# Loading x as float16 through GpSimd's queue and reordering the first loads of a state-space and feed-forward kernel

## The chip, the core and the metric

The kernel runs on one core of a Trainium2 chip. The metric is the device time of one execution in microseconds (us); lower is better. The time before is a median of 125.82 us over 3 runs (125.32 to 125.95). The profile is of one execution on that core.

The names of the engines in the profile: PE is TensorE's matmul and PEld its weight load, DVE is VectorE, ACT is ScalarE, POOL is GpSimd and SP is SyncE, which does nothing here but issue transfers. A "q" behind the name (SPq, POOLq) is the engine's sequencer, issuing or waiting.

## The reference

Two layers, one behind the other. The first is a chunked state-space scan over 4 batches, 8 heads and 768 tokens, with a head dimension of 32 and a state of 16. The second is a bilinear feed-forward over all 3072 tokens, with a model width of 256 and an inner width of 1536.

```
log_a = log(clip(a, 1e-6, 1))
for each chunk c of the sequence:
    cum   = cumsum(log_a of the chunk)
    L     = exp(cum_i - cum_j), causal
    y     = ((C B^T) * L) x  +  (C state) * exp(cum_i)
    state = exp(sum log_a) * state + sum_j exp(cum_last - cum_j) B_j x_j
X   = y as (batch * token, head * dim)           # 3072 x 256
out = ((X w_a) * (X w_b)) w_out                  # 3072 x 256, float32
```

All inputs and the output are float32 in DRAM. The inputs x, B and C lie as (batch, head, token, element), so one token of one head is a contiguous run of 128 bytes of x and of 64 bytes of B or C.

## The kernel before, in words

**Work items.** The kernel cuts the 768 tokens into 6 blocks of Q = 128 tokens and the 4 batches into 2 pairs of batches. A "pair" p, from 0 to 11, is one block of two batches: block p // 2, batches 2 (p % 2) and the next one. Pairs 0 to 3 (p below P0 = 4) hold two neighbouring tokens of a head on one partition, so their x comes in runs of 256 bytes and each pair is loaded by two transfers of 64 partitions each, one for each batch (`load1`). Pairs from 4 on hold one token on each of 128 partitions, and one transfer loads the whole pair (`load2`).

**A pair's steps.** The decay factors come from scans over a (`scan`, `factors`). `scale_bc` multiplies B and C of a pair by them into float16 tiles bm and cm. For pairs 0 to 3 PE transposes them (`transposes`, evacuated by ACT into bt and by DVE into ct); from pair 4 on they go into a tile "planes", which a transposing DMA on SP turns (`turn`, tile "turned"). `scores` multiplies C and B on PE, `mask` multiplies the scores by the causal mask on DVE (or, with `by_pool`, ACT copies them to tmp and POOL multiplies), and the float16 result t is the moving operand of `pv_u`, whose stationary operand is the pair's x in float16, the tile X16. `ds_mm` multiplies bm and X16 into the state's increment; `state_sums` (DVE) and `state_spread` (POOL: tiles spair or sbd, and gU) carry the state on. Pairs 0 to 3 go through `pv`; from pair 4 on both pairs of a block go through `outputs` in `group(blk)`.

**x.** Before the change x is loaded as float32 (tile xn) and `scale_x` makes X16 from it, multiplying by XS = 1024: on ACT for pairs 0, 1, 2, 5 and 6 and on POOL for pairs 3, 4 and 7 to 11. Evacuations of y multiply by YS / XS, with YS = 16, to undo the factor.

**Feed-forward.** `unit` (pairs 0 to 3, 256 tokens at a time) and `bunit` (a block of 512 tokens) multiply Wa and Wb with y on PE into the PSUM tiles aps and bps; ACT copies aps into asb and DVE multiplies bps and asb into hk or hkb; `out_mm` or `bout` multiplies that with Wo, ACT evacuates into osb and SP stores it. The weights are float32 in DRAM and arrive as float16 by transfers that POOL issues, in two halves each (`load_w`, `load_wo`): half 0 of Wa and Wb in the head of the program, half 1 and Wo later.

**What sets the order.** Nothing is scheduled by a compiler (`tc.manual_schedule()`): each engine runs its instructions in the order in which the program text issues them, and waits on semaphores for what others make. A transfer is an instruction of the engine that issues it: SP, ACT or POOL. So a load in POOL's list is issued only when POOL has done everything that stands ahead of it, and holds up what stands behind it for as long as its issue takes. The built program uses eight semaphores in turn for transfers of SP and ACT together, and eight for those of POOL; a transfer waits for the one that used its semaphore before.

**The head.** SP and ACT issue a and the loads of pair 0, a table ch (head and parity masks) and a table c32; POOL makes sel, ident and causal, then issues three of the four loads of B and C of pair 1, Wa and Wb half 0, and both loads of x of pair 1. PE runs warm-up matmuls on zeros (`warmup`, tile warm) between the steps of pair 0. The feed-forward starts with `unit_mm(0, 0, Wa)`: L600 in the profile, the first instruction to need a weight.

**Later loads.** `loads_bc` issues C and B of a pair on SP. x of pairs 3, 4, 6, 7, 9, 10 and 11 is issued on SP, and of pairs 2, 5 and 8 on POOL. `prep(p)` is `scale_bc` of both on POOL, then `turn`; `prep_x(p)` is `scale_x` on POOL.

Of the kernel before, what the change touches and what calls it, by code (L numbers as in the profile page):

```python
# [10 lines left out]
f32 = mybir.dt.float32  # L11
f16 = mybir.dt.float16
# [16 lines left out]
def kernel(  # L29
# [34 lines left out]
    for b in range(nb):  # L64
        p32[b * H : (b + 1) * H, 128 + b * NG : 128 + (b + 1) * NG] = 1.0
    p32_t = nc.inline_tensor(p32, "p32")
    ph = np.zeros((128, H + 2), np.float32)
    ph[:, 0:H] = (j[:, None] // N) == np.arange(H)[None, :]
    ph[:, H:] = (j[:, None] // N) % 2 == np.arange(2)[None, :]
    ph_t = nc.inline_tensor(ph, "ph")  # L70

    const = ctx.enter_context(tc.tile_pool(name="const", bufs=1))
    c32 = const.tile([BH, p32.shape[1]], f32, name="c32")
    ch = const.tile([128, H + 2], f32, name="ch")
    ident = const.tile([128, 128], f16, name="ident")
    causal = const.tile([128, 2, Q], f16, name="causal")
    sel = const.tile([BH, 2, NBP, H], f32, name="sel")
    indm = c32[:, 0:128]
    selb = c32[:, 128 : 128 + nb * NG]
    headm = ch[:, 0:H]  # L80
    par = ch[:, H:]

    big = ctx.enter_context(tc.tile_pool(name="big", bufs=1))
    a_sb = big.tile([BH, NBLK, Q], f32, name="a_sb")
# [21 lines left out]
    G = big.tile([128, nb, NG], f32, name="G")  # L106

    inp = ctx.enter_context(tc.tile_pool(name="inp", bufs=3))
    mid = ctx.enter_context(tc.tile_pool(name="mid", bufs=4))
    ffh = ctx.enter_context(tc.tile_pool(name="ffh", bufs=4))  # L110
    hkb = ctx.enter_context(tc.tile_pool(name="hkb", bufs=2))
# [9 lines left out]


    pair_in = {}
    banks = iter(BANKS)

    def bank(name):
# [3 lines left out]
    def tiles(p):  # L130
        Bn = inp.tile([128, H, 2, N], f32, name="bn", tag="bn")
        Cn = inp.tile([128, H, 2, N], f32, name="cn", tag="cn")
        Xn = inp.tile([128, H, 2, D], f32, name="xn", tag="xn")
        pair_in[p] = (Bn, Cn, Xn)

    def by_token(t_):
        return t_.rearrange("p h r n -> p (h r n)").rearrange("p (t h n) -> p t h n", t=2, h=H)
# [1 line left out]
    def load1(eng, p, which, bt, i0=0, n=64):  # L139
        blk, bp = divmod(p, NBP)  # L140
        if p >= P0:
            return eng.dma_start(
                by_token(pair_in[p][which])[:, bt],
                (B, C, x)[which][2 * bp + bt, :, blk * Q : (blk + 1) * Q, :].rearrange("h q n -> q h n"),
            )
        src = (B, C, x)[which][2 * bp + bt, :, blk * Q + 2 * i0 : blk * Q + 2 * i0 + 2 * n, :]
        return eng.dma_start(  # L147
            pair_in[p][which][64 * bt + i0 : 64 * bt + i0 + n].rearrange("i h r n -> i h (r n)"),
            src.rearrange("h (i r) n -> i h (r n)", r=2),
        )  # L150

    def load2(eng, p, which):
        if p < P0:
            return [load1(eng, p, which, bt) for bt in range(2)]
        blk, bp = divmod(p, NBP)
        return eng.dma_start(  # L156
            by_token(pair_in[p][which]).rearrange("p t h n -> p (t h) n"),
            (B, C, x)[which][2 * bp : 2 * bp + 2, :, blk * Q : (blk + 1) * Q, :].rearrange("t h q n -> q (t h) n"),
        )

    def load_w(half):
        c = slice(half * KC, (half + 1) * KC)
        return [
            nc.gpsimd.dma_start(W[half], src.rearrange("(f p) e -> p f e", p=128)[:, :, c])
            for W, src in ((Wa, moe_w_a), (Wb, moe_w_b))
        ]
# [14 lines left out]
    nc.sync.dma_start(ch, ph_t.ap())  # L181
    load1(nc.scalar, 0, 1, 0, 32, 32)
    nc.scalar.preload_act_table_set("natural_log_exp_and_others")
    load1(nc.scalar, 0, 2, 1)
    load1(nc.sync, 0, 2, 0)
    load1(nc.sync, 1, 0, 0)
    nc.sync.dma_start(c32, p32_t.ap())
    nc.vector.memset(warm.bitcast(u32), 0)
    nc.vector.memset(zero, 0.0)
# [11 lines left out]
    nc.gpsimd.affine_select(  # L201
        out=ident, in_=ident, compare_op=ALU.is_equal, fill=0.0, base=0, pattern=[[-1, 128]], channel_multiplier=1
    )
    nc.gpsimd.memset(causal, 1.0)
    for bt in range(2):
        v = causal[64 * bt : 64 * bt + 64]
        nc.gpsimd.affine_select(
            out=v, in_=v, compare_op=ALU.is_ge, fill=0.0, base=0, pattern=[[-1, 2], [1, Q]], channel_multiplier=-2
        )
    load1(nc.gpsimd, 1, 0, 1)  # L210
    load1(nc.gpsimd, 1, 1, 0)
    load1(nc.gpsimd, 1, 1, 1)
    load_w(0)
    for bt in range(2):
        load1(nc.gpsimd, 1, 2, bt)

    def warmup(n, bank, cols=512):
        for _ in range(n):
            nc.tensor.matmul(
                bank[:, 0:cols], warm[:, 0:128], warm[:, 0:cols], start=True, stop=True, skip_group_check=True  # L220
            )
# [53 lines left out]
    def flat(f, lo, hi):  # L275
        return f[:, lo:hi].rearrange("p k r b h -> p (k r b h)")


    st = {}

    def scale_x(p, eng):
        X16 = mid.tile([128, H, 2, D], f16, name="x16", tag="x16")
        xo, xi = X16.rearrange("p h r d -> p (h r d)"), pair_in[p][2].rearrange("p h r d -> p (h r d)")
        st.setdefault(p, {})["X16"] = X16
        if eng is nc.scalar:
            nc.scalar.mul(xo, xi, XS)
        else:
            eng.tensor_scalar(xo, xi, XS, None, ALU.mult)  # L288

    def scale_bc(p, which, eng, factor=None):  # L290
        blk, bp = divmod(p, NBP)
# [276 lines left out]
    def state_spread(p):  # L568
        blk, bp = divmod(p, NBP)
        if p + NBP < P0:  # L570
            Sbd = mid.tile([128, 2, H * D], f16, name="sbd", tag="sbd")
            nc.gpsimd.tensor_tensor(
                out=Sbd.rearrange("p t (m c) -> p t m c", m=4),
                in0=U32[:, p].unsqueeze(2).broadcast_to((128, 2, 4, 2 * D)),
                in1=maskbd.rearrange("p (m e) d -> p m (e d)", e=2).unsqueeze(1).broadcast_to((128, 2, 4, 2 * D)),
                op=ALU.mult,
            )
        else:
            Sbd = mid.tile([128, 2, 2 * D], f16, name="spair", tag="spair")
            nc.gpsimd.tensor_tensor(  # L580
                out=Sbd.rearrange("p t (e d) -> p t e d", e=2),
                in0=U32[:, p].rearrange("p t (e d) -> p t e d", e=2),
                in1=par.unsqueeze(1).unsqueeze(3).broadcast_to((128, 2, 2, D)),
                op=ALU.mult,
            )
        if blk + 1 < NG:
            nc.gpsimd.tensor_tensor(
                out=gU[:, p + NBP],
                in0=U32[:, p],
                in1=G[:, 2 * bp : 2 * bp + 2, blk + 1].unsqueeze(2).broadcast_to((128, 2, 2 * D)),  # L590
                op=ALU.mult,
            )
        st.setdefault(("S", p + NBP), {})["Sbd"] = Sbd
# [117 lines left out]
            for w in (1, 0):  # L711
                load2(nc.sync, p, w)

    def loads_x(p, eng=None):
        if p < NP:
            load2(eng or nc.gpsimd, p, 2)

    def fb(k):
        nc.vector.reciprocal(flat(fB, k, k + 1), flat(fC, k, k + 1))

# [27 lines left out]
    mask(product0(0, 0))  # L748
    mask(product0(0, 1))
    mask(product0(1, 1), by_pool=True)  # L750
    scale_x(0, nc.scalar)
    mask(product0(1, 0))
    warmup(5, tcp)
    scale_bc(1, 1, nc.vector)
    scale_bc(1, 0, nc.gpsimd)
    py = [bank("py0"), bank("py1")]
    pv_u(0, 0, py, True)
    for bt in range(2):
# [12 lines left out]
    scan(5, NBLK)  # L771
    over_mid(1, NBLK)
    sel_over_mid(1, NBLK, nc.vector)
    warmup(2, tcp)
    aps = [unit_mm(0, 0, Wa), unit_mm(0, 1, Wa)]
    asb = [evac_a(aps[0])]
    scores(1)
# [3 lines left out]
    asb.append(evac_a(aps[2]))  # L781
    fps = bank("fps")
    factors(1, 3, fps)
    scale_x(1, nc.scalar)
    for m in range(3):
        mask(product(1, m))
    bps = [unit_mm(0, k2, Wb) for k2 in range(3)]
# [11 lines left out]
    )  # L799
    load_wo(1)  # L800
    tiles(3)
    for bt in range(2):
        load1(nc.gpsimd, 2, 2, bt)
    times(0, 0, bps[0], asb[0])
    pv(1, DS=(0, SC[:2]), split=True)
    ds_mm(0, 64, SC[:2])
# [15 lines left out]
    state_spread(1)  # L822
    for t_ in planes:
        nc.gpsimd.memset(t_[:, 0:4].bitcast(u32), 0)
    nc.gpsimd.memset(causal_q, 1.0)
    nc.gpsimd.affine_select(
        out=causal_q, in_=causal_q, compare_op=ALU.is_ge, fill=0.0, base=0, pattern=[[1, Q]], channel_multiplier=-1
    )
# [1 line left out]
    tc.add_manual_dep(b3[0].ins, w1[1].ins.name, AFTER, reason="weights ahead of pair 3's inputs")  # L830
    for bt in range(2):
        load1(nc.sync, 3, 1, bt)
    loads_x(3, nc.sync)
    loads_bc(4)
    go((0, 3), (0, 4), (1, 3), (0, 5))
    transposes(2, apart=True)
# [5 lines left out]
    mask(product(2, 1))  # L842
    mask(product(2, 2))
    h()
    scale_x(2, nc.scalar)
    scale_bc(3, 0, nc.gpsimd)
    scale_bc(3, 1, nc.gpsimd)
    scale_x(3, nc.gpsimd)
    loads_bc(5)
    o = [bank("ops"), bank("ops")]  # L850
    out_mm(0, 0, o[0], range(6))
# [13 lines left out]
    def prep(p, spread=()):  # L865
        if p < NP:
            scale_bc(p, 1, nc.gpsimd)
            scale_bc(p, 0, nc.gpsimd)
            turn(p)
        for q in spread:  # L870
            if q // NBP < NBLK - 1:
                state_spread(q)

    def prep_x(p):
        if p < NP:
            scale_x(p, nc.gpsimd)

    def group(blk):
        for p in range(blk * NBP, (blk + 1) * NBP):
# [31 lines left out]
    prep(4, (2,))  # L911
    for f in stores:
        f()
    loads_x(4, nc.sync)
    loads_x(5)
    prep(5)
    tiles(6)
    load2(nc.sync, 6, 1)
# [11 lines left out]
    state_sums(3)  # L930
    fb(3)
    state_spread(3)
    prep_x(4)
    go((2, 3), (2, 4), (2, 5))
    out_half(2, 0)
    o_ps = bank("ops")
# [1 line left out]

    scores(4)
    mask(product(4, 3), by_pool=True, by_token=True)  # L940
    scale_x(5, nc.scalar)
    prep(6)
    masked(4, (0, 1))
    out_mm(2, 1, o_ps, range(6, NK))
# [3 lines left out]
    scores(5)  # L948
    mask(product(5, 3), by_pool=True, by_token=True)
    mask(product(5, 2), by_pool=True, by_token=True)  # L950
    loads_x(6, nc.sync)
    prep(7)
    loads_x(7, nc.sync)
    loads_bc(8)
    masked(5, (0, 1), *pu(3, 2, 3, 4, 5))
    group(2)
# [2 lines left out]

    stage(6, True, (4, 5))  # L960
    loads_x(8)
    prep_x(7)
    masked(6, (0, 1))
    masked(6, (2,), *bu(2, 0, 1, 2))
    scale_x(6, nc.scalar)
    bgo(2, 3, 4)
    stage(7, True)
    loads_bc(9)
    prep(8)
    prep(9)  # L970
    loads_x(9, nc.sync)
    loads_bc(10)
    masked(7, (0, 1, 2), *bu(2, 5, 6, 7, 8, 9, 10, 11))
    group(3)
# [1 line left out]
    bout(2, 1)  # L976

    stage(8, True, (6, 7))
    prep_x(8)
    prep_x(9)  # L980
    prep(10)
    loads_bc(11)
    loads_x(10, nc.sync)
    masked(8, (0, 1))
    masked(8, (2,), *bu(3, 0, 1, 2, 3, 4, 5))
    for blk in range(4, NBLK):
        pB = blk * NBP + 1
        stage(pB, False)
        if blk > 4:
            prep_x(pB)  # L990
        loads_x(pB + 2, nc.sync)
        prep(pB + 2)
        masked(pB, (0, 1))
        bout(blk - 2, 2)
        masked(pB, (2, 3), *bu(blk - 1, 6, 7, 8, 9))
        group(blk)
        bout(blk - 2, 3)
        bgo(blk - 1, 10, 11)
        if blk + 1 < NBLK:
            stage(pB + 1, False, (pB - 1, pB))  # L1000
            prep_x(pB + 1)
            masked(pB + 1, (0, 1))
            bout(blk - 1, 0)
            masked(pB + 1, (2,))
            bout(blk - 1, 1)
            masked(pB + 1, (3,), *bu(blk, 0, 1, 2, 3, 4, 5))
# [40 lines left out]
```

## Time and profile before

| what | value |
|---|---|
| median of 3 runs | 125.82 us |
| span of the profiled execution, first to last instruction | 124.2 us |
| what lies around the span (median less span) | 1.6 us |
| first weight matmul starts | 11.59 us |
| mean granted clock of TensorE | 0.998 |
| DMA, mean rate | 111 GB/s |

The profile's page gives the busy time of each engine with its share of the span, the span in 40 slices (each digit the busy share in tenths), the DMA queues, the chain of work that ended last and the costliest groups of instructions. A group's line has the source line, the engine, the operation, the output and inputs by the program's names, the count and the duration of one. Lists of waits have the waiting engine and line, what ended the wait, and the total in us, the number of waits and the longest. A timeline's line has the start, the duration, and in brackets the idle time before it and what ended that. For transfers, the time "to landing" runs from the start of the issue to the last semaphore increment.

### The profile page before, as it was taken

How to read it: one execution, taken by the hardware profiler on the slowest of the kernel's cores; microseconds unless marked ns; L12 is line 12 of the kernel's file. 1: busy time of each engine (PE TensorE's matmuls, PEld its weight loads, DVE VectorE, ACT ScalarE, POOL GpSimd, SP SyncE). 2: the span in 40 equal slices, each digit the busy share in tenths (PEclk: the TensorE clock that was granted, in tenths of full speed). 3: DMA queues.
4: the chain of work that ended last, by engine and by line, in shares of the span. 5: the costliest groups of instructions: out<-in, count | busy, mean ns of one | idle time of the engine just before them, and what ended most of it. 6: DMA issues, size and time to landing. Idle time of an engine off the chain costs nothing.

```text
span 124.2 us, 3750 instructions
## 1 busy us (share of the span) xinstructions
PE 117.6 (95%) x1471; PEld 79.9 (64%) x1471; DVE 85.4 (69%) x162; ACT 71.6 (58%) x142; POOL 64.2 (52%) x109
## 2 busy tenths in 40 slices
PE   5887999999999998999999999999999999999990
PEld 2444788988888886844457456657464775555890
DVE  1886787885978589399983989848789544747200
ACT  0464845784645684788658755683637746657220
POOL 7999699947992479467735768114920000000000
PEclk9999999999999999999999999999999999999999
DMA  3999999997989699999886797369831012010122
GB/s 66 169 154 232 171 190 132 206 154 78 98 109 224 98 97 184 110 162 134 103 136 97 54 133 135 64 68 132 176 122 48 0 42 84 5 42 0 42 84 84
DMA packets 64753, 13.73 MB, mean 111 GB/s; under 512 B 59568, under 2 KB 64336, under 8 KB 64736
## 3 DMA queue, kind: packets, MB, share of 16 engines
q1 hardware_dynamic: 60528, 9.27, 48.8%
q0 software_dynamic: 2208, 3.87, 17.8%
q10 hardware_dynamic: 2000, 0.36, 1.6%
q8 instruction: 11, 0.18, 0.6%
q14 instruction: 6, 0.05, 0.1%
HBM read 11.13 MB, written 3.15 MB: 115 GB/s over the span
## 4 chain that ended last, share of the span: by engine, by line
PE 63%; DMA 17%; POOL 7%; SPq 7%; issue 3%; DVE 1%; ACT 1%; POOLq 0%; ACTq 0%; DVEq 0%
PE ops L693 15%; PE aps L666 13%; PE bps L666 13%; DMA bn<-in_B_dram 8%; PE aps L600 6%; PE bps L600 5%; DMA Wa<-in_moe_w_a_dram 5%; PE ops L636 4%; SPq L347 4%; DMA turned<-planes 3%; SPq L156 3%; POOL bm L303 1%; PE SC L357 1%; POOL cn L147 1%; PE SC L432 1%
## 5 line engine op out<-in xcount | busy, mean ns | idle before, releaser
L614 ACT COPY asb<-aps 128x512 f32<-128x512 f32 x72 | 41.9, 586 | 15.0 <-PE aps L666 9.7
L678 DVE TENSOR_TENSOR hkb<-bps,asb 128x512 f16<-128x512 f32 x48 | 32.3, 687 | 12.9 <-ACT asb L614 11.8
L666 PE MATMUL aps<-XB,Wa 128*128 128x512 f16 x96 | 28.6, 379 | 0.0
L666 PE MATMUL bps<-XB,Wb 128*128 128x512 f16 x96 | 28.5, 379 | 0.0
L693 PE MATMUL ops<-Wo,hkb 128*128 128x256 f16 (+1 forms) x204 | 22.5, 267 | 0.0
L693 PEld LDWEIGHTS <-hkb 128*128 128x128 f16 x204 | 18.5, 98 | 3.1
L412 DVE TENSOR_TENSOR t<-SC,causal_q 128x512 f16<-128x512 f32 x26 | 16.6, 681 | 5.1 <-PE SC L357 5.1
L621 DVE TENSOR_TENSOR hk<-bps,asb 128x512 f16<-128x512 f32 x24 | 16.1, 683 | 3.5 <-ACT asb L614 3.1
L666 PEld LDWEIGHTS <-Wb 128*128 128x128 f16 x96 | 9.9, 103 | 11.0 <-issue 0.3
L666 PEld LDWEIGHTS <-Wa 128*128 128x128 f16 x96 | 9.7, 103 | 9.1 <-issue 0.2
L600 PE MATMUL aps<-X2T,Wa 128*128 128x256 f16 x96 | 14.3, 274 | 1.0 <-DMA Wa<-in_moe_w_a_dram 0.7
L705 ACT ACTIVATE osb<-ops 128x256 f32<-128x256 f32 (+1 forms) x16 | 6.0, 376 | 14.4 <-PE ops L693 14.2
L600 PE MATMUL bps<-X2T,Wb 128*128 128x256 f16 x96 | 14.1, 273 | 0.0
L288 POOL TENSOR_SCALAR x<-xn 128x512 f16<-128x512 f32 x7 | 10.4, 1489 | 6.1 <-DMA xn<-in_x_dram 5.9
L636 PE MATMUL ops<-Wo,hk 128*128 128x256 f16 x96 | 11.6, 273 | 0.0
L600 PEld LDWEIGHTS <-Wa 128*128 128x128 f16 x96 | 9.3, 104 | 2.5 <-DMA Wa<-in_moe_w_a_dram 1.2
L600 PEld LDWEIGHTS <-Wb 128*128 128x128 f16 x96 | 9.8, 103 | 0.7
L636 PEld LDWEIGHTS <-hk 128*128 128x128 f16 x96 | 8.9, 98 | 1.5 <-DVE hk L621 0.2
L412 DVE TENSOR_TENSOR t<-SC,causal 128x512 f16<-128x512 f32 x13 | 8.2, 682 | 1.8 <-PE SC L372 1.7
L303 POOL TENSOR_TENSOR bm<-bn,fB 128x256 f16<-128x256 f32 x11 | 7.0, 640 | 4.6 <-DMA bn<-in_B_dram 2.8
L410 POOL TENSOR_TENSOR t<-tmp,causal_q 128x512 f16<-128x512 f32 x6 | 6.9, 1159 | 3.7 <-ACT tmp L409 3.6
L295 POOL TENSOR_TENSOR planes<-cn,fC 128x256 f16<-128x256 f32 x8 | 5.0, 623 | 7.2 <-DMA cn<-in_C_dram 7.0
(94 smaller groups left out, 118.2 us busy)
## 6 DMA issues: line engine op xcount, KB each, us to landing
out_dram<-osb SPq DMA_DIRECT2D x23, 128.0 KB, 1.9
xn<-in_x_dram SPq DMA_DIRECT2D x6, 256.0 KB, 4.9
cn<-in_C_dram SPq DMA_DIRECT2D x8, 128.0 KB, 4.0
bn<-in_B_dram SPq DMA_DIRECT2D x8, 128.0 KB, 4.3
Wa<-in_moe_w_a_dram POOLq DMA_DIRECT2D x2, 384.0 KB, 6.9
Wb<-in_moe_w_b_dram POOLq DMA_DIRECT2D x2, 384.0 KB, 8.2
Wo<-in_moe_w_out_dram POOLq DMA_DIRECT2D x2, 384.0 KB, 6.8
xn<-in_x_dram POOLq DMA_DIRECT2D x4, 128.0 KB, 7.3
```

The source lines that it names most:

```text
L288: eng.tensor_scalar(xo, xi, XS, None, ALU.mult)
L303: eng.tensor_tensor(out=m_, in0=raw, in1=(f[:, blk, :, bp] if factor is None else factor).unsqueeze(3).broadcast_to((128, 2, H, N)), op=AL ...
L410: nc.gpsimd.tensor_tensor(out=o_, in0=tmp, in1=c_, op=ALU.mult)
L412: nc.vector.tensor_tensor(out=o_, in0=i_, in1=c_, op=ALU.mult)
L600: nc.tensor.matmul(ps[:, kk * 2 * Q : (kk + 1) * 2 * Q], W[k // 6][:, f, k % 6 // 3 * 384 : (k % 6 // 3 + 1) * 384].rearrange("p (c kk) -> ...
L614: (nc.vector.tensor_copy if on_dve else nc.scalar.copy)(asb, a_ps)
L621: nc.vector.tensor_tensor(out=s["hk"][:, 2 * k2 : 2 * k2 + 2, :].rearrange("p k q -> p (k q)"), in0=b_ps, in1=asb, op=ALU.mult)
L636: nc.tensor.matmul(o_ps[:, 0:d_model], hk[:, k, bt * Q : (bt + 1) * Q], Wo[:, k, :], start=(k == 0), stop=(k == NK - 1), skip_group_check= ...
L666: nc.tensor.matmul(t_, W[k // 6][:, f, k % 6 // 3 * 384 : (k % 6 // 3 + 1) * 384].rearrange("p (c kk) -> p kk c", kk=3)[:, k % 3], XB[:, b ...
L678: return lambda: nc.vector.tensor_tensor(out=s["hk"][:, k], in0=ps[1], in1=asb, op=ALU.mult)
L693: nc.tensor.matmul(o_ps[:, 0:w], hk[:, k, c * Q : (c + 1) * Q], Wo[:, k, cs], start=(k == 0), stop=(k == NK - 1), skip_group_check=True,)
L705: nc.scalar.activation(out=o_sb[:, 0:w], in_=o_ps[:, 0:w], func=AF.Copy, scale=1.0 / (YS * YS))
```

## The change

- x goes from DRAM to SBUF as float16 by transfers that POOL issues, straight into X16, without the factor. `scale_x`, `prep_x` and the float32 tile xn are gone. X16 has a pool of its own with 6 buffers.
- The factor XS sits in the masks instead: causal and causal_q are filled with XS, the head mask in ch is multiplied by XS, and a second parity mask with XS (parx) is used for the state; the parity mask par, which the B planes use, keeps its ones.
- In POOL's list of the head x of pair 0 and then Wa and Wb half 0 stand ahead of the causal mask, and x of pair 1 behind it. All four loads of B and C of pair 1 go to SP and ACT, in the places that x of pair 0 and one load of B had.
- bm of pair 1 is made on DVE instead of POOL.
- The two warm-up matmuls ahead of the first weight matmul are gone.
- All later loads of x are issued on POOL, at the places shown below.

```diff
-    ph = np.zeros((128, H + 2), np.float32)
-    ph[:, 0:H] = (j[:, None] // N) == np.arange(H)[None, :]
-    ph[:, H:] = (j[:, None] // N) % 2 == np.arange(2)[None, :]
+    ph = np.zeros((128, H + 4), np.float32)
+    ph[:, 0:H] = XS * ((j[:, None] // N) == np.arange(H)[None, :])
+    ph[:, H : H + 2] = (j[:, None] // N) % 2 == np.arange(2)[None, :]
+    ph[:, H + 2 :] = XS * ph[:, H : H + 2]
...
+    xin = ctx.enter_context(tc.tile_pool(name="xin", bufs=6))
...
-        Xn = inp.tile([128, H, 2, D], f32, name="xn", tag="xn")
-        pair_in[p] = (Bn, Cn, Xn)
+        X16 = xin.tile([128, H, 2, D], f16, name="x16", tag="x16")
+        pair_in[p] = (Bn, Cn, X16)
...
+    def loads_x(p):
+        if p < NP:
+            load2(nc.gpsimd, p, 2)
...
-    load1(nc.scalar, 0, 2, 1)
-    load1(nc.sync, 0, 2, 0)
+    load1(nc.scalar, 1, 0, 1)
     load1(nc.sync, 1, 0, 0)
+    load1(nc.scalar, 1, 1, 1)
+    load1(nc.sync, 1, 1, 0)
...
-    nc.gpsimd.memset(causal, 1.0)
+    loads_x(0)
+    w0 = load_w(0)
+    nc.gpsimd.memset(causal, XS)
...
-    load1(nc.gpsimd, 1, 0, 1)
-    load1(nc.gpsimd, 1, 1, 0)
-    load1(nc.gpsimd, 1, 1, 1)
-    load_w(0)
-    for bt in range(2):
-        load1(nc.gpsimd, 1, 2, bt)
+    loads_x(1)
...
-    def scale_x(p, eng):
...
-                in1=par.unsqueeze(1).unsqueeze(3).broadcast_to((128, 2, 2, D)),
+                in1=parx.unsqueeze(1).unsqueeze(3).broadcast_to((128, 2, 2, D)),
...
-    scale_x(0, nc.scalar)
...
-    scale_bc(1, 0, nc.gpsimd)
+    scale_bc(1, 0, nc.vector)
...
-    warmup(2, tcp)
...
-    scale_x(1, nc.scalar)
...
-    nc.gpsimd.memset(causal_q, 1.0)
+    nc.gpsimd.memset(causal_q, XS)
...
-    loads_x(3, nc.sync)
+    loads_x(3)
...
-    scale_x(2, nc.scalar)
...
-    scale_x(3, nc.gpsimd)
...
-    loads_x(4, nc.sync)
-    loads_x(5)
...
     state_spread(3)
-    prep_x(4)
+    loads_x(4)
+    loads_x(5)
...
-    scale_x(5, nc.scalar)
...
-    loads_x(6, nc.sync)
     prep(7)
-    loads_x(7, nc.sync)
+    loads_x(6)
+    loads_x(7)
...
-    prep_x(7)
...
-    scale_x(6, nc.scalar)
...
-    loads_x(9, nc.sync)
+    loads_x(9)
...
-    prep_x(8)
-    prep_x(9)
     prep(10)
     loads_bc(11)
-    loads_x(10, nc.sync)
+    loads_x(10)
...
-        if blk > 4:
-            prep_x(pB)
-        loads_x(pB + 2, nc.sync)
         prep(pB + 2)
+        loads_x(pB + 2)
...
-            prep_x(pB + 1)
```

More of the change, by code (lines that the diff above doesn't have):

```diff
@@ L73 @@
     c32 = const.tile([BH, p32.shape[1]], f32, name="c32")
-    ch = const.tile([128, H + 2], f32, name="ch")
+    ch = const.tile([128, H + 4], f32, name="ch")
     ident = const.tile([128, 128], f16, name="ident")
@@ L80 @@
     headm = ch[:, 0:H]
-    par = ch[:, H:]
+    par = ch[:, H : H + 2]
+    parx = ch[:, H + 2 :]
     big = ctx.enter_context(tc.tile_pool(name="big", bufs=1))
@@ L123 @@
     pair_in = {}
+    st = {}
     banks = iter(BANKS)
@@ L132, in tiles @@
         Cn = inp.tile([128, H, 2, N], f32, name="cn", tag="cn")
-        Xn = inp.tile([128, H, 2, D], f32, name="xn", tag="xn")
-        pair_in[p] = (Bn, Cn, Xn)
+        X16 = xin.tile([128, H, 2, D], f16, name="x16", tag="x16")
+        pair_in[p] = (Bn, Cn, X16)
+        st.setdefault(p, {})["X16"] = X16
     def by_token(t_):
@@ L276, in flat @@
         return f[:, lo:hi].rearrange("p k r b h -> p (k r b h)")
-    st = {}
-    def scale_x(p, eng):
[L282 to L288, printed above, removed]
     def scale_bc(p, which, eng, factor=None):
@@ L712, in loads_bc @@
                 load2(nc.sync, p, w)
-    def loads_x(p, eng=None):
-        if p < NP:
-            load2(eng or nc.gpsimd, p, 2)
     def fb(k):
@@ L801 @@
     tiles(3)
-    for bt in range(2):
-        load1(nc.gpsimd, 2, 2, bt)
+    loads_x(2)
     times(0, 0, bps[0], asb[0])
@@ L872, in prep @@
                 state_spread(q)
-    def prep_x(p):
-        if p < NP:
-            scale_x(p, nc.gpsimd)
     def group(blk):
```

## The prediction

> **What bounds the kernel now.** I read the page first, then who PE waited for, then the chain of waits through the head, then short stretches of the head, then the DMA issues. From the page:
>
> ```profile
> span 124.2 us, 3750 instructions
> PE 117.6 (95%) x1471; PEld 79.9 (64%) x1471; DVE 85.4 (69%) x162; ACT 71.6 (58%) x142; POOL 64.2 (52%) x109
> PEclk9999999999999999999999999999999999999999
> ```
>
> PE is busy for 95% at the full granted clock; ACT and POOL, whose scaling goes away, have slack of some 50 and 60 us. The median of the runs is 125.82 us, so 1.6 us lie around the span; I sum against the span and add 1.6. What PE waited for from 11 us to the end:
>
> ```profile
> PE aps L600 <- DMA Wa<-in_moe_w_a_dram: 0.7, 1, 0.7
> PE SC L418 <- POOL t L410: 0.5, 1, 0.5
> PE aps L600 <- DVE X2T L492: 0.3, 1, 0.3
> PE SC L357 <- DMA turned<-planes: 0.2, 1, 0.2
> ```
>
> So once the feed-forward starts, PE loses under 1 us altogether: 0.47 at 49.5 us, 0.28 at 16.5, 0.16 at 68.0 by the timeline. Everything else behind the head is PE work that the change leaves as it is. The head, by the chain:
>
> ```profile
> 3.74 1.35 POOL cn L147 x2
> 5.10 6.44 DMA Wa<-in_moe_w_a_dram
> 11.54 0.05 issue
> 11.59 1.05 PE aps L600 x8
> ```
>
> GpSimd issues Wa's first half only at 5.10, behind its masks and three loads of pair 1; it lands at 11.54 and PE starts at 11.59. What PE could have done without that wait (timeline of PE):
>
> ```profile
> 10.03 0.29 PE L325 MATMUL SC<-ident,bm 128*128 128x128 f16 x2 [0.16 <-POOL bm L303]
> 10.15 0.27 PE L325 MATMUL SC<-ident,cm 128*128 128x128 f16 x2
> 10.26 0.59 PE L219 MATMUL tc<-warm 128*128 128x512 f16 x2
> 11.59 1.05 PE L600 MATMUL aps<-X2T,Wa 128*128 128x256 f16 x8 [0.73 <-DMA Wa<-in_moe_w_a_dram]
> ```
>
> Pair 1's transposes end at 10.42; the two warm-ups behind them (removed by the change) are only cover for the wait. The ceiling of the head is 11.59 - 10.42 = 1.17 us. But the DMA engines (last but one column: their busy share in the stretch) are full:
>
> ```profile
> 3.00:4.00 1.00, 1.00 (x5) 0.38 (x3) 0.78 (x4) 1.00 (x1) 1.00 (x2) 1.00 0.70 108
> 4.00:5.00 1.00, 1.00 (x13) 0.55 (x11) 0.97 (x3) 0.22 (x1) 1.00 (x2) 1.00 0.97 128
> 6.00:7.00 1.00, 0.79 (x37) 0.51 (x35) 0.74 (x2) 0.73 (x3) 1.00 (x2) 1.00 1.48 208
> 8.00:9.00 1.00, 0.89 (x19) 0.34 (x18) 1.00 (x2) 0.40 (x2) 0.94 (x1) 1.00 0.97 166
> ```
>
> **Step 1, the weights' issue.** POOL's order becomes sel, ident, two loads of x(0), Wa, Wb, the causal mask, two loads of x(1). ident ends at 1.74; a load of x from POOL took 0.73 us of POOL each. So x(0) is issued 1.74 to 3.20, Wa at 3.20 (1.9 earlier), Wb at 3.95. The mask's 0.31 + 0.86 follow and end near 5.9; DVE first needs it at 7.21, a cover of 1.3. x(1) is issued 5.9 to 7.4, and POOL is free for its mask product at 7.4 (before: 8.0). Bounds for Wa's landing. If it keeps its 6.44 us: 9.64, and PE's own work decides. If the engines simply finish all that is queued ahead: unused capacity from 3 to 5 us is 0.30 + 0.03, and some 0.1 before 3, so Wa lands some 0.4 earlier, at 11.1. The bytes ahead of it are the same: x(0), 256 KB, changes places with 192 KB of B and C of pair 1 on POOL's queue, and the hardware queues carry 256 KB of B and C where they had 256 KB of x and 64 KB of B. I take 11.0, near the second bound, since the rows of 5 to 11 us show engines at 1.0 and more. PE's start is then 11.05, a gain of 0.55.
>
> The Trainium skill, DMA: Bandwidth & Descriptors, section "Issuing engines are not separate DMA queues", says that transfers from all issuing engines run on the same 16 DMA engines, so another queue saves only issue time. It speaks against a gain here; taken to its end Wa would land where it did and the head would gain nothing, and only the unused share of 3 to 5 us stands against it.
>
> **Step 2, what else must be there.** Wb landed 13.63 and was used at 14.06, 2.47 behind PE's start; by the same 0.4 it comes at 13.2 and is needed at 11.05 + 2.47 = 13.5: covered by 0.3, and if late it caps the head's gain near 0.4. x(1) landed 14.07 and 14.49 before ACT's 0.63 of scaling; queued behind Wb it lands near 14.2, needed at 15.48 - 0.55 = 14.9: covered by 0.7. x(0), issued at 1.74 and 2.47, by the 3.3 of bn and 4.3 of cn on that queue lands by 6.8; PE wants it near 7.9, and DVE's second mask (to 8.47) is late next, so dropping scale_x(0) gains nothing. The B and C of pair 0 landed 2.6 to 3.2 after issue, the last at 5.1, and DVE multiplies C at 5.35: a cover of 0.25, which x(0)'s traffic from 3.4 may eat (0 to 0.2 lost). ACT issues pair 1's second half of C, and in the built program that DMA waits for ACT's first C of pair 0 (4.74): it ends at 5.4, ahead of the evacuation at 5.81. C of pair 1 then lands, by 4.1 to 4.6 us, at 8.9 to 9.4; DVE wants it at 9.01 and then makes bm(1) too (0.45 more on DVE, taken from POOL's 0.80). So pair 1's transposes end between 10.4 and 10.9, before Wa. Cost nothing, but the real ceiling is about 0.8.
>
> **Step 3, the scaling.** Removed: seven on POOL (10.4 us) and five on ACT (5 x 0.63 = 3.2 us). Added on POOL: six loads of 256 KB (pairs 4, 6, 7, 9, 10, 11) at 1.22, four of 128 KB at 0.73, less three of B and C and bm(1): about +7.2. POOL's sum falls by some 3 us and ACT's by 3.2, beside PE: worth only the two stalls. At 49.5 PE waits for pair 5's product on POOL; ahead of it stood scale_x(4) (1.49, itself 3.36 late) and bm(6) waiting for B at 45.9. SP loses pair 3's two x issues (3.67 us), so B and C of pairs 4 to 7, the turned planes 4 and 5, and all behind them come some 2 us sooner; t of pair 4 starts near 42.5 instead of 43.7, pair 5's products end near 47.7 instead of 49.5. That is 1.8 against a stall of 0.47: it goes; late next is PE itself. At 68.0 PE waits for turned planes of pair 8, held by B landing at 62.9; SP no longer issues x(6), x(7) ahead of it: 0.16 goes. The 0.28 at 16.5 stays (DVE's evacuation, 0.43, directly behind PE). Between 0 and 0.63 then; I take 0.6.
>
> **Step 4, x late.** x(4) and x(5) now go out behind pair 3's state, near 38.8 and 40.0; x from POOL in 256 KB took 5.5 and 5.9 us, so x(5) is there at 45.9 and PE reads it at 48.5 - 0.55 = 48.0: covered by 2.1. x(6) to x(11) have more. No trace of before has a casting load of short rows; its price lies between that by bytes and that by rows of the weights, which cast. Wb landed 2.09 after Wa, for 768 KB read in 256 rows: x(0), 256 KB in 1024 rows, costs 0.70 by bytes and 8.4 by rows. The uncast x(1) took 0.86 behind Wb on that queue, rows and bytes alike; I take 0.86.
>
> The same page of the Trainium skill gives, in its section "Specifications", 512 B as the least transfer at line rate, with a read-modify-write below. The cast rows of 64 and 128 B fall under it; no row here shows such a cast.
>
> **Sum.** 124.2 - 0.55 - 0.6 = 123.0, and 1.6 around it: 124.6 us. (0.5%, 0.63 us, is about what a measurement of this kernel can tell from no change.) Its own range: head 0.2 to 0.8, stalls 0.3 to 0.63: 124.3 to 125.3.
>
> **Rivals.**
> - Full overlap: Wa lands before 10.4 because GpSimd's queue takes its share of the engines from the hardware queues. For it: issue is 1.9 earlier. Against: shares of 1.0. Head 1.1, all stalls 0.9: 123.8.
> - The weights gain nothing, as the engines are full: only the stalls go. For it: the stretches from 5 us on. 125.82 - 0.6 = 125.2; if POOL's order keeps the 0.47 too, 125.6.
> - Slower: a casting load is paid by rows. Place: x(0) ahead of Wa on the same queue. At half of the weights' row price x(0) takes 4.2 instead of 0.86, Wa lands at 14.3, PE starts 2.8 later than before, less 0.6: 128.0; x(5) would be late too. It decides (slower by 0.63) from 2.6 us for x(0) (1.8 more than forecast, 0.55 + 0.6 + 0.63), some 41 ns a row on an engine. Against it: uncast rows of the same length on the same queue cost 13 (0.86 x 16 / 1024).
>
> **Chances.** Forecast 0.52, full overlap 0.12, weights gain nothing 0.20, paid by rows 0.14, and 0.02 for a head that loses by B and C of pair 0. Faster: 0.52 + 0.12 + a quarter of 0.20 = 0.69. Same: 0.15. Slower: 0.16. The range runs from the full overlap's 123.6 to 126.3, which takes in the no-gain case and a casting load up to 2.5 us, and leaves out most of the row-priced case and a little below.
>
> **What would show it.** Right: the first aps L596 of the changed kernel starts near 11.0 and waits for Wa, not Wb; PE no longer waits for POOL's product before group 2's reads of it (the 0.5 us row above); POOL's busy sum near 61 and ACT's near 68 with PE's waits behind 12 us down to about 0.3. Wrong: Wa landing past 11.5, packets of x on POOL's queue of a row each, PE waiting for x_ at pair 0, or at group 2 near 48 us.

## The result, and the profile after

| | before | after |
|---|---|---|
| median of 4 runs each, one chip | 125.88 us (125.32 to 126.37) | 131.03 us (129.40 to 132.63) |
| profiled execution: time, span | 125.82, 124.2 us | 129.97, 128.3 us |
| first weight matmul starts | 11.59 us | 14.78 us |
| mean granted clock | 0.998 | 0.973 |

The ratio after / before is 1.031 [1.022, 1.039]: the change makes the kernel slower. Every ratio here and below leaves out executions more than 1.5% above the fastest of the same kernel; of after these are two of the four (132.1 and 132.63 us, at clocks of 0.957 and 0.956), so the median above lies over what the ratio says of the other two (129.40 and 129.97 us).

From the page of after (span; busy times; granted clock by slices of 3.2 us; the two largest DMA queues with packets, MB and share of 16 engines):

```profile
span 128.3 us, 3723 instructions
PE 119.2 (93%) x1469; PEld 80.7 (63%) x1469; DVE 85.7 (67%) x163; ACT 69.3 (54%) x137; POOL 60.7 (47%) x108
PEclk9968779999999999999999999999999999999999
q0 software_dynamic: 22496, 4.20, 40.8%
q1 hardware_dynamic: 47088, 7.37, 40.7%
```

PE does two instructions less than before and is busy 1.6 us longer: the clock line shows why, it falls in slices 3 to 6. GpSimd's queue (q0) had 2208 packets and 17.8% before; it now has ten times as many. What PE waited for from 11 us on:

```profile
PE SC L321 <- DVE bm L299: 2.6, 1, 2.6
PE aps L596 <- DVE X2T L488: 0.3, 1, 0.3
PE SC L353 <- DMA turned<-planes: 0.2, 1, 0.2
```

The rows for Wa (0.7) and for POOL's product (0.5) are gone. In the place of the first stands pair 1's transposes waiting for bm. DVE makes bm behind cm, so the row names the nearer releaser; the timeline of after shows the one behind it:

```profile
6.16 0.42 DVE L299 TENSOR_TENSOR cm<-cn,fps 128x256 f16<-128x256 f32 x1 [0.77 <-DMA cn<-in_C_dram]
6.64 0.29 PE L321 MATMUL tc<-ident,cm 128*128 128x128 f16 x2 [0.84 <-DVE cm L299]
...
13.55 0.42 DVE L299 TENSOR_TENSOR cm<-cn,fC 128x256 f16<-128x256 f32 x1 [3.45 <-DMA cn<-in_C_dram]
13.90 0.42 DVE L299 TENSOR_TENSOR bm<-bn,fB 128x256 f16<-128x256 f32 x1
14.37 0.40 PE L321 MATMUL SC<-ident,bm 128*128 128x128 f16 x2 [2.65 <-DVE bm L299]
```

DVE stood idle for 3.45 us until C of pair 1 landed, and for 0.77 us, earlier, until C of pair 0 did. The chain of waits says the same (start, duration, what):

```profile
1.54 3.10 DMA cn<-in_C_dram
4.65 8.81 DMA cn<-in_C_dram
14.37 0.61 PE SC L321 x4
14.98 1.71 PE aps L596 x8
```

A 64 KB load that ACT issues at 4.65 lands at 13.46. In before the two loads of C of pair 1 took 4.28 and 4.36. The weights, meanwhile, were early: Wa landed at 9.74 (11.54 before) and Wb at 12.15 (13.63).

The clock in short stretches of after (the number behind POOL's):

```profile
7.00:8.00 1.00, 0.79 (x35) 0.59 (x33) 0.71 (x2) 0.26 (x2) 0.43 (x1) 0.67 1.09 172
8.00:9.00 1.00, 1.00 (x13) 0.41 (x4) 0.78 (x2) 0.59 (x1) 0.06 (x1) 0.50 1.12 172
...
14.00:15.00 1.00, 0.63 (x6) 0.57 (x7) 0.84 (x3) 0.00 (x0) 0.00 (x0) 0.58 1.23 219
15.00:16.00 1.00, 1.00 (x6) 0.75 (x5) 0.92 (x3) 0.97 (x3) 0.00 (x0) 0.50 1.09 197
16.00:17.00 1.00, 1.00 (x36) 0.53 (x33) 0.31 (x1) 0.46 (x1) 0.00 (x0) 0.50 0.89 205
17.00:18.00 1.00, 1.00 (x32) 0.52 (x16) 0.62 (x2) 0.63 (x2) 0.00 (x0) 0.71 0.10 29
```

By these shares PE runs at half clock from 14.16 to 17.58, that is for 2.8 us from the start of the first weight matmul, after 2.65 us without work. An earlier stretch at half clock, from about 7.3 on (rows 7.00 and 8.00), lies ahead of the wait for C of pair 1; between PE's first matmul, at 1.26, and this stretch PE had no wait longer than 0.84 us.

**Where the 4.1 us of span went**, by how much later the same PE instruction starts in after than in before:

| step | us |
|---|---|
| pair 1's transposes start (10.03 to 14.37) | +4.35 |
| from there to the first weight matmul: no wait for Wa, no warm-ups (1.56 to 0.41) | -1.16 |
| half clock on the first weight matmuls (difference 3.19 at their start, 4.42 at 17.9) | +1.23 |
| group 2: no wait for POOL's product | -0.64 |
| pair 7's turned planes late (+0.23), less 0.12 of drift ahead of it | +0.11 |
| pair 8's turned planes in time | -0.22 |
| last output transfer (2.91 to 3.31 behind the last matmul) | +0.40 |
| sum | 4.07 |

### The profile page after: what moved, and what is told of

Read it like the earlier page. It is cut to its first block, busy times and chain, and to the rows that moved or that the text cites. A ratio compares the mean times of both kernels' runs of the same rounds, so it can differ in the third digit from the quotient of the medians.

```text
span 128.3 us, 3723 instructions
## 1 busy us (share of the span) xinstructions
PE 119.2 (93%) x1469; PEld 80.7 (63%) x1469; DVE 85.7 (67%) x163; ACT 69.3 (54%) x137; POOL 60.7 (47%) x108
## 3 DMA queue, kind: packets, MB, share of 16 engines
q0 software_dynamic: 22496, 4.20, 40.8%
## 4 chain that ended last, share of the span: by engine, by line
PE 80%; DMA 14%; DVE 1%; ACT 1%; issue 1%; ACTq 1%; SPq 0%; DVEq 0%
PE ops L689 17%; PE aps L662 15%; PE bps L662 15%; PE aps L596 9%; DMA cn<-in_C_dram 9%; PE bps L596 8%; PE ops L632 7%; DMA turned<-planes 5%; PE SC L353 2%; PE SC L414 2%; PE SC L368 1%; PE SC L428 1%; PE SC L321 1%; PE fps L255 1%; PE SC L503 1%
## 5 line engine op out<-in xcount | busy, mean ns | idle before, releaser
L662 PEld LDWEIGHTS <-Wb 128*128 128x128 f16 x96 | 9.9, 103 | 10.9
L596 PE MATMUL aps<-X2T,Wa 128*128 128x256 f16 x96 | 15.4, 288 | 0.3 <-DVE X2T L488 0.3
L662 PEld LDWEIGHTS <-Wa 128*128 128x128 f16 x96 | 9.7, 103 | 9.1 <-issue 0.2
L596 PEld LDWEIGHTS <-Wa 128*128 128x128 f16 x96 | 9.8, 108 | 1.8 <-DVE X2T L488 0.4
L161 POOL DMA_DIRECT2D x<-in_x_dram x8 | 9.5, 1189 | 0.0
L299 POOL TENSOR_TENSOR bm<-bn,fB 128x256 f16<-128x256 f32 x10 | 6.2, 624 | 3.5 <-PE aps L596 1.9
## 6 DMA issues: line engine op xcount, KB each, us to landing
out_dram<-osb SPq DMA_DIRECT2D x23, 128.0 KB, 1.8
cn<-in_C_dram SPq DMA_DIRECT2D x8, 128.0 KB, 5.7
bn<-in_B_dram SPq DMA_DIRECT2D x8, 128.0 KB, 5.9
x<-in_x_dram POOLq DMA_DIRECT2D x8, 128.0 KB, 6.1
```

The lines of the kernel that those rows point to most:

```text
L161: return eng.dma_start(by_token(pair_in[p][which]).rearrange("p t h n -> p (t h) n"), (B, C, x)[which][2 * bp : 2 * bp + 2, :, blk * Q : ( ...
L299: eng.tensor_tensor(out=m_, in0=raw, in1=(f[:, blk, :, bp] if factor is None else factor).unsqueeze(3).broadcast_to((128, 2, H, N)), op=AL ...
L596: nc.tensor.matmul(ps[:, kk * 2 * Q : (kk + 1) * 2 * Q], W[k // 6][:, f, k % 6 // 3 * 384 : (k % 6 // 3 + 1) * 384].rearrange("p (c kk) -> ...
L662: nc.tensor.matmul(t_, W[k // 6][:, f, k % 6 // 3 * 384 : (k % 6 // 3 + 1) * 384].rearrange("p (c kk) -> p kk c", kk=3)[:, k % 3], XB[:, b ...
```

## The experiments

Theory A: weights that are issued early on GpSimd's queue keep the DMA engines from the short rows of B and C on the hardware queues; C lands late and PE with it. Theory B: the casting load of x(0), paid by rows, is what holds the engines. The times of before on the two chips used were 124.76 and 125.47 us; every ratio of this section is against those.

**e1: weights back behind the loads of B and C.** After, with the weights' first half issued behind the masks and three loads of B and C of pair 1 ahead of them on POOL, as in before. x is still cast, x(0) still first on POOL's queue.

```diff
-    load1(nc.scalar, 1, 0, 1)
-    load1(nc.scalar, 1, 1, 1)
-    load1(nc.sync, 1, 1, 0)
...
     loads_x(0)
-    w0 = load_w(0)
...
+    load1(nc.gpsimd, 1, 0, 1)
+    load1(nc.gpsimd, 1, 1, 0)
+    load1(nc.gpsimd, 1, 1, 1)
+    w0 = load_w(0)
     loads_x(1)
```

> The changed kernel with x of pair 0 and 1 still cast on POOL's queue, but Wa and Wb half 0 back behind the masks, and three loads of B and C of pair 1 back on POOL ahead of them. Theory A (the early weights on POOL's queue keep the engines from the short rows of B and C of pair 1 on the hardware queues): C of pair 1 lands by 9.5 instead of 13.46, PE's first weight matmul starts at 12.0 to 12.5, time 125.3 to 126.3. Theory B (the casting rows of x(0), paid by the row, are the loss): pair 0's C stays at 6.1, PE starts past 13.5 and the time stays above 128.

125.75 us, ratio 1.007 [1.003, 1.011]. C of pair 1 landed at 7.69 and 8.46, Wa at 11.63. From the timeline of PE in e1:

```profile
11.47 0.28 PE L321 MATMUL SC<-ident,bm 128*128 128x128 f16 x2
11.59 0.28 PE L321 MATMUL SC<-ident,cm 128*128 128x128 f16 x2
11.70 1.25 PE L596 MATMUL aps<-X2T,Wa 128*128 128x256 f16 x8
```

No wait stands in front of the transposes. Putting the weights back takes nearly all of the loss away, although x(0) is cast as in after: A holds, and B is at most a small part. (e1 also puts three loads of B and C back on GpSimd's queue, so it does not part the weights' place from the queue of those loads; e2 and e5 leave them on SP and ACT.) What is left of B: pair 0's last C landed at 5.95 (5.12 in before), and pair 0's transposes of cm started 0.68 late. The transposes of pair 1 came at 11.47 instead of 10.03. Only part of that is the late C: DVE makes both cm and bm of pair 1 now, behind its masks, and the five warm-ups ahead took 2.31 us, as long as at half clock in after, against 1.25 in before, although the profile gives a clock of 1.00 here. From the timelines of DVE and PE in e1, and of PE in before:

```profile
10.04 0.95 DVE L299 TENSOR_TENSOR cm<-cn,fC 128x256 f16<-128x256 f32 x1
10.91 0.41 DVE L299 TENSOR_TENSOR bm<-bn,fB 128x256 f16<-128x256 f32 x1
```

```profile
8.05 2.31 PE L226 MATMUL tc<-warm 128*128 128x512 f16 x5
```

```profile
7.00 1.25 PE L219 MATMUL tc<-warm 128*128 128x512 f16 x5
```

Further on, PE gained 0.64 at group 2 and 0.23 at pair 8, and lost 0.54 here:

```profile
PE SC L353 <- DMA turned<-planes: 0.5, 1, 0.5
```

By this profile e1 ends level with the profiled execution of before (its last matmul starts at 121.05, before's at 121.06), which took 125.82 us; on e1's chip before took 124.76, so the 0.7% of its runs are not located in it.

**e2: early weights without a casting load ahead of them.** x(0) as float32 on ACT and SP with a copy on ACT, the weights first on POOL's queue (issued at 1.71), B and C of pair 1 on SP and ACT.

```diff
+    load1(nc.scalar, 0, 2, 1)
+    load1(nc.sync, 0, 2, 0)
     load1(nc.scalar, 1, 0, 1)
...
-    loads_x(0)
     w0 = load_w(0)
```

> The changed kernel with x of pair 0 loaded as float32 on ACT and SP in its old place and copied to float16 on ACT; the weights stay early, B and C of pair 1 stay on SP and ACT, now behind x(0). Theory A: C of pair 1 lands at 13 or later as before, and x(0) too is starved, PE's first weight matmul starts at 14.5 or later, time 129 to 132. Theory B: pair 0's C lands at 5.1 again, PE starts by 12, time 125 to 126.

128.96 us, ratio 1.036 [1.028, 1.043]. There is no cast ahead of the weights (x of pair 1 is still cast behind them, issued from 4.65 on), and the loss is as large. Timeline of DVE and of PE in e2:

```profile
8.20 0.42 DVE L305 TENSOR_TENSOR cm<-cn,fps 128x256 f16<-128x256 f32 x1 [2.51 <-DMA cn<-in_C_dram]
...
13.89 0.42 DVE L305 TENSOR_TENSOR cm<-cn,fC 128x256 f16<-128x256 f32 x1 [1.71 <-DMA cn<-in_C_dram]
```

```profile
14.94 1.04 PE L602 MATMUL aps<-X2T,Wa 128*128 128x256 f16 x8
```

With the weights 1.56 us earlier still (Wa landed at 7.55, Wb at 10.05), even C of pair 0, issued at 2.05 and 2.23, landed at 7.74 and 8.12 instead of 4.95 and 5.12. This is the clean evidence; C of pair 1 also stood behind x(0) here, and its second load was issued only at 8.14. A is right a second time, and B's expectation missed by 3 us.

**e5: the same weights in shorter rows.** The question is how the engines share themselves. If they take the queues in turn, packet by packet (A1), a hardware queue gets one row of 128 B for each weight row of 1536 B, and shorter weight rows help B and C at the same bytes. If they serve GpSimd's queue first or share by bytes (A2), shorter rows change nothing. After, with Wa's and Wb's first halves as three transfers of 256 columns each, all still ahead of the mask.

```diff
-    w0 = load_w(0)
+    load_w3(Wa, moe_w_a)      # for g in range(3): 256 columns of half 0, nc.gpsimd.dma_start
+    load_w3(Wb, moe_w_b)
```

> The changed kernel with Wa and Wb half 0 each issued as three transfers of 256 columns, so each weight row on POOL's queue is 1024 B read instead of 3072; POOL issues for 2.8 us longer. Theory A1 (an engine takes its queues in turn, one packet of each, and a packet of the hardware queues is one row of 128 B): B and C of pair 1 get three times the turns while the weights move, C of pair 1 lands at 10 to 11.5 instead of 13.46, PE's first weight matmul at 11.8 to 13. Theory A2 (POOL's queue simply goes first, or the engines are shared by bytes): C lands at 13 or later and PE starts at 14.5 or later.

Two runs, 130.02 and 128.08 us, too few for an interval; the landings, from the profile of the first, are what it was for. The DMA queues from 6.5 to 8.5 us (packets, MB, share), in after:

```profile
q0 software_dynamic: 195, 0.29, 86.4%
q1 hardware_dynamic: 266, 0.03, 16.2%
q10 hardware_dynamic: 305, 0.04, 13.6%
```

and in e5:

```profile
q0 software_dynamic: 480, 0.23, 87.3%
q1 hardware_dynamic: 641, 0.09, 36.5%
q10 hardware_dynamic: 464, 0.06, 21.5%
```

In both, each hardware queue moves 1.0 to 1.6 packets for one of GpSimd's, whatever its size: 266 / 195 and 305 / 195 in after, 641 / 480 and 464 / 480 in e5. When GpSimd's packets shrink to a third, the hardware queues move 1105 packets instead of 571 in the same 2 us, and GpSimd's bytes fall only from 0.29 to 0.23 MB. This is an average, and no strict turn is shown, since the profile does not list packets by engine: in after the ratio is 0.7 and 1.0 from 10 to 11 us (101 and 137 for 139) and over 4 from 8 to 9 us (303 and 309 for 72), and in before q1 moved 441 for 126 from 6.5 to 8.5 us. C of pair 1 landed at 9.11 and 10.19 (12.58 and 13.46), the weights as soon as before the split (Wa's last third at 9.77, Wb's at 12.00). PE, from its timeline in e5:

```profile
12.09 0.28 PE L331 MATMUL SC<-ident,cm 128*128 128x128 f16 x2
12.20 1.04 PE L606 MATMUL aps<-X2T,Wa 128*128 128x256 f16 x8
```

2.6 us sooner than in after. A1's landings and start came, A2's did not. The six issues spread the weights from 3.26 to 7.50 us, but GpSimd's queue kept its share (87.3% against 86.4%), so the weights did not simply stand aside. The Trainium skill, DMA: Bandwidth & Descriptors, section "Queues, rings and completion order", says that a DMA engine goes round the queues it has work for, a packet at a time; these counts agree with that in the average, and add that the short row pays. The page has some 9 to 17 descriptors as typical of a packet; on the hardware queues here the trace has one row to a packet. The six issues cost elsewhere: DVE waited 1.2 us for the mask that POOL makes behind them. PE also stood for 2.3 us at 16.8, named only "issue"; the profile of e10, an execution of 128.20 us with whole weight rows, has such a wait of 2.0 us in the same group of matmuls, so it is not put down to this edit.

The same count tells what the change did to B and C of pair 1. On GpSimd's queue, as in before, such a 64 KB load goes out in 16 packets of 4096 B: e1 moved its three between 5.9 and 8.0 us in 48 packets over 2 KB, 0.20 MB. On the queues of SP and ACT it is 512 rows of 128 B, a packet each. If the engines share by packets, the move from GpSimd's queue gave each of these loads 32 times as many turns to wait for.

**e6: the clock alone.** After, with warm-up matmuls put in the two gaps of the head: four long ones instead of a short one in pair 0's transposes, and eleven long ones instead of a short one ahead of pair 1's.

```diff
-    transposes(0, [tb, tcp], lambda: warmup(1, SC[3], 128))
+    transposes(0, [tb, tcp], lambda: warmup(4, SC[3]))
...
-    warmup(1, tcp, 128)
+    warmup(11, tcp)
```

> The changed kernel with three more warm-up matmuls of 512 columns between pair 0's transposes and eleven instead of a short one ahead of pair 1's. If the granted clock of 0.5 from 14.16 to 17.57 is a cost of its own (2.8 us of bound PE work at half rate, 1.4 us), the granted clock is 1.00 throughout, PE's first weight matmul still starts near 14.6 and the time falls by 1.2 to 1.6, to 128.0 to 128.6, with runs closer together. If the wait for C alone counts, the time stays at 129.4 or more.

128.85 us (128.62 to 129.00), ratio 1.032 [1.026, 1.037], span 127.3. From its page, and what PE waited for behind 11 us:

```profile
PEclk9999999999999999999999999999999999999997
```

```profile
PE SC L321 <- DVE bm L299: 1.4, 1, 1.4
```

The wait for C is partly covered by warm-ups and ends no sooner: the first weight matmul starts at 15.04, 0.26 later than in after. Yet the span is 1.0 shorter. PE from there to the same later matmuls, in after and in e6:

```profile
14.78 1.92 PE L596 MATMUL aps<-X2T,Wa 128*128 128x256 f16 x8
...
17.91 0.42 PE L267 MATMUL fps<-selr,Pr 32*64 32x16 f32 x8
```

```profile
15.04 1.04 PE L596 MATMUL aps<-X2T,Wa 128*128 128x256 f16 x8
...
17.05 0.42 PE L267 MATMUL fps<-selr,Pr 32*64 32x16 f32 x8
```

After takes 3.13 us for this stretch, e6 2.01 and before 1.89. So the half clock costs after 1.12 us against e6 and 1.24 against before, which is the 1.23 of the table above. The earlier half-clock stretch of after is gone in e6 too and PE still waits for C, so that one cost nothing that shows. The times do not show the gain: e6's ratio, 1.032, is no lower than after's 1.031 with its wide interval. The expected 128.0 to 128.6 went by after's time on a chip where before took 125.88 us; where e6 ran, before took 124.76. Its runs do lie closer together, as expected.

**e11: x(0) uncast on the same queue.** Why was pair 0's C late in e1? The order of e1, with x(0) as plain float32 on POOL's queue and a copy on ACT. If casting rows are what costs, C of pair 0 lands as in before.

```diff
# against e1
-        pair_in[p] = (Bn, Cn, X16)
+        Xn = inp.tile([128, H, 2, D], f32, name="xn", tag="xn") if p < 1 else X16
+        pair_in[p] = (Bn, Cn, Xn)
...
+    copy_x(0)                 # nc.scalar.copy(X16, xn)
```

> The order of loads of the run with the weights behind B and C, with x of pair 0 in the same place on POOL's queue but as float32 with a copy on ACT: the same bytes read in the same rows, no cast. If the cast is paid by the row (32 ns a row of 128 B written), the uncast rows travel in packets of 4096 B, and the last C of pair 0 lands at 5.2 to 5.5 instead of 5.95. If any traffic of 256 KB there costs the same, it lands at 5.9 or later.

127.73 us as a median of 8 runs that lie far apart (125.12 to 129.23), ratio 1.006 [0.999, 1.012] from three of them: no verdict on the time. Pair 0's last C landed at 6.48, later than behind the casting load (5.95), and PE in the head waited for it:

```profile
PE tc L326 <- DVE cm L304: 1.0, 1, 1.0
```

The expectation from the row price falls. An uncast x goes out in packets of 4096 B, 200 ns each in the median, against 32 ns for a casting row. That the longer packet holds the short rows up more would follow from sharing by packets; it is not shown. In these single executions it is the load's place, on GpSimd's queue and issued at 1.71, and not its cast, that costs pair 0 its C.

**e4, e8, e10: what the change is worth without its head.** e4 has before's head and casts x from pair 2 on; e8 also casts pair 1, behind the weights; e10 is e8 with x of pair 7 issued later, just ahead of that of pair 8, since pair 7's turned planes came late beside the casts of pairs 6 and 7 (6.33 us to landing in after).

```diff
# e8 against after (e4: p < 2, loads of x(1) uncast as in before)
+        Xn = inp.tile([128, H, 2, D], f32, name="xn", tag="xn") if p < 1 else X16
...
+    load1(nc.scalar, 0, 2, 1)
+    load1(nc.sync, 0, 2, 0)
...
-    loads_x(0)
-    w0 = load_w(0)
...
+    load1(nc.gpsimd, 1, 0, 1)
+    load1(nc.gpsimd, 1, 1, 0)
+    load1(nc.gpsimd, 1, 1, 1)
+    w0 = load_w(0)
     loads_x(1)
...
-    scale_bc(1, 0, nc.vector)
+    scale_bc(1, 0, nc.gpsimd)
...
+    warmup(2, tcp)
```

> The head of the kernel before (x of pairs 0 and 1 as float32 with a copy on ACT, order of loads, warm-ups), and casting loads on POOL from pair 2 on. Both theories put the loss in the head: PE's first weight matmul at 11.6, and behind it PE loses its 0.47 on POOL's product: 125.2 to 125.5. A third theory (casting rows cost engine time all the way and hold the later B and C) expects 125.9 or more.

> The head of the kernel before, with x of pair 0 as float32 and a copy on ACT; x of pair 1 and all later ones cast on POOL, pair 1's behind the weights. If casting rows are harmless where nothing short waits behind them, x(1) lands by 14.6 against a need at 15.5, PE starts at 11.6, the stall on POOL's product at 49.5 is gone, and the time is 0.4 to 0.8 below the kernel before, ratio 0.993 to 0.997. If they hold B and C of later pairs or the turned planes, ratio 1.000 or more.

> The run before it with the load of x of pair 7 moved behind pair 6's product on POOL, 6 us later. In the changed kernel the turned planes of pair 7 took 6.3 us to land beside x(6) and x(7) and PE lost 0.2 there. If the casting rows hold the transposing transfer, the planes land in 4 to 5 us, that stall goes, and the time is 0.2 to 0.4 lower than with x(7) early; if not, the two times agree within 0.2.

| | median us | ratio | what its profile shows |
|---|---|---|---|
| e4 | 125.29 | 1.001 [0.997, 1.005] | PE waits 1.3 for the copy of x(1), whose load landed at 15.9 and 16.3 |
| e8 | 124.88 | 0.995 [0.992, 0.998] | first weight matmul at 11.26, x(1) landed at 13.54 and 14.02 |
| e10 | 124.68 | 0.997 [0.993, 1.000] | pair 7's planes took 6.42 from issue to landing (4.10 in e8) |

The three profiles are of executions of 126.44, 126.04 and 128.20 us, above their kernels' medians, so what they show need not hold for the runs behind the ratios. e8 is faster than before by 0.2 to 0.8%, as expected, and so than both kernels. Waits of PE in e8 behind 11 us:

```profile
PE bps L602 <- ACT asb L616: 0.6, 1, 0.6
PE SC L434 <- POOL t L412: 0.4, 1, 0.4
PE aps L602 <- DVE X2T L494: 0.3, 1, 0.3
PE aps L602 <- DMA Wa<-in_moe_w_a_dram: 0.2, 1, 0.2
```

The stall of 0.5 at group 2 is gone (group 2's matmuls, about 48 to 50 us, run without a wait), and two small ones, at 21 and 30 us, stand in this one execution instead, so the gain is shown by the times and not by this profile. e10's gain was not there: its median lies within 0.2 us of e8's, and in its profiled execution the planes landed no sooner. What holds pair 7's planes stays open. So does e4 against e8: their intervals overlap, and if there is a difference, its cause is not shown.

## Why the prediction was wrong

It said 124.6 us, within 123.6 to 126.3, and gave "slower" 0.16. The step that failed is **step 2: the landing of C of pair 1**, "by 4.1 to 4.6 us, at 8.9 to 9.4". It landed at 13.46, after 8.81 us. The 4.1 to 4.6 were read from loads that had hardly any weights beside them: in before, C of pair 1 and the weights stood on one queue, C ahead and in packets of 4096 B. The change puts them on different queues, where they run abreast and C goes row by row, and e5 shows at what rate: 1.0 to 1.6 short rows for each weight row. The text moved the weights past three loads on POOL's queue and priced that for the weights alone; the sentence "cost nothing, but the real ceiling is about 0.8" should have had the price of those loads beside the weights.

- **Step 1** put Wa's landing between 9.64 and 11.1 and took 11.0, because the engines are full; Wa landed at 9.74, at the bound it did not take. The engines were full as said, but GpSimd's queue took its share from the others. That is the mechanism of the full-overlap rival (Wa before 10.4), which counted the share as free. The gain was there: 1.16 between the transposes and the weight matmul, out of the ceiling of 1.17. The skill's rule quoted in step 1, that another queue saves issue time alone, held for Wa to the letter: issued 1.83 earlier, it landed 1.80 earlier. The text took it to speak against a gain; it says nothing of which load lands first, and C of pair 1 took 4.5 us longer from issue to landing.
- **Step 2, pair 0's C**: "0 to 0.2 lost" was 0.96 of landing and 0.82 of PE's start on cm. In e1, with that C at 5.95 and bm of pair 1 on DVE, pair 1's transposes start at 11.47, so an early Wa would have gained little there; the forecast had them end by 10.9. How much of it is the late C and how much the slower PE of that execution is not parted. Wb, x(0) and x(1) were in time, as forecast: Wb 12.15, x(0) 6.43, x(1) 13.82.
- **Missing: the clock.** The head's waits were priced at their length only. PE's idle time was followed by 3.4 us at half clock, 1.23 us more, and e6, which fills the gap, has neither. The sum has no such term. The two warm-ups that the change removes stood behind this wait and would not have filled it.
- **Step 3 was right in its mechanism**: 0.64 at group 2 and 0.22 at pair 8 went, the 0.28 stayed, against 0.6 forecast and 0.63 as the most; POOL's sum is 60.7 and ACT's 69.3 (61 and 68 forecast). It did not see the 0.23 at pair 7's planes.
- **Step 4**: 0.86 was taken for casting x(0). The trace's packets are rows of 128 B at 32 ns, so 1024 x 32 / 16 = 2.05 us of 16 engines, below the 2.6 us from which the "paid by rows" rival decides. That rival had the right sign and the wrong cause: e2 has no such load ahead of the weights and is as slow, and in e11, with it uncast, pair 0's C lands no sooner. The price set against that rival, 13 ns for an uncast row, was no price of a row: such loads go out 4096 B to a packet.
- **The rivals.** The nearest to what decided had 0.02, as "a head that loses by B and C of pair 0", without a price; B and C of pair 1 behind the weights were no rival at all.

## What to carry to other kernels

When a load is moved to another queue or past others, price what then runs abreast of it, not only the load itself: a queue of short rows next to a queue of long ones moved 1.0 to 1.6 rows for each long one here, so a small load that something waits for belongs ahead of the weights, on their queue, or the weights' rows must be cut. Read a load's duration only from rows that had the same company. A longer wait of PE can cost the clock behind it too, so price that, or keep warm-ups there until the wait is gone. Where the limit lies no run here measures: a wait of 2.65 us was followed by half clock, the 1.35 us left in e6 were not, and the earlier half-clock stretch of after came without a wait over 0.84 us between PE's first matmul and it.

## What the runs showed of the hardware

- The engines' sharing between queues went by packets and not by bytes, in the average of 2 us: weights cut to a third in row length landed as soon (9.77 and 12.00, against 9.74 and 12.15), and the loads of C beside them 3.3 to 3.5 us sooner.
- The same 64 KB load of rows of 128 B is 16 packets of 4096 B on GpSimd's queue (e1) and 512 packets on that of SP or ACT.
- A casting load moves one row to a packet (q0: 2208 packets in before, 22496 in after), while uncast rows of x on the same queue go out 4096 B to a packet. The queue's share of the engines rose from 17.8% of 124.2 us to 40.8% of 128.3 us, and the only waits of PE listed from group 2 on in after and e1 are those of 0.2 and 0.5 us for pair 7's planes.
- 2.65 us without work on PE were followed by 3.4 us at half clock; with warm-ups in the gap (e6) the clock stayed at 1.00 and the stretch behind it was 1.12 us shorter.
